# Later rows asked for sooner, twelve of sixteen weight conversions a step later, and the scores of two stacked blocks moved behind the products of the step ahead

## The chip, the cores and the metric

The kernel runs on one core of a Trainium2 chip. The time is that of one execution on the device, in microseconds, and the smaller one is the better one. The core has a matrix engine (TensorE, PE in the profile), a vector engine (VectorE, DVE), a scalar engine (ScalarE, ACT), a general engine (GpSimd, POOL) and a queue of DMA issues (SyncE, SP). Each of them runs its own list of instructions in order; they meet through semaphores.

## The reference

The reference is an attention with decay, followed by two layers of a feed-forward kind. What is computed, cut to what matters:

```python
# q, k, v: 4 batches, 8 heads, 576 positions, 64 wide; f: 4 x 8 x 576
scores = scale * np.matmul(q, k.transpose(0, 1, 3, 2))
cum = np.cumsum(np.log(np.clip(f, 0.0001, 1.0)), axis=-1)
scores = np.where(causal, -1e9, scores + cum[:, :, :, None] - cum[:, :, None, :])
attn = np.exp(scores - max); attn = attn / (sum + 1e-09)
x = attn @ v                                  # as 2304 tokens x 512
x = np.maximum(x @ w_in, 0.0) ** 2 @ w_out    # first layer pair, 2048 wide
h = x @ w_in2
out = np.where(h > 0, h, np.exp(np.minimum(h, 0)) - 1) @ w_out2
```

## The kernel before

The attention of batch 0 is computed in 20 steps (`todo`): eight steps of kind A, one for each head, for the first part of the positions; then for each pair of heads a step "4", in which the last 64 positions of both heads are stacked into one block of scores (`soft_4`), and two steps B for the positions between (`soft_b`). Each step has a front half, `soft`: scores on TensorE, a reduction on VectorE (`reduce_min`, L446), an exponential on ScalarE (`expo`, L449). Its back half, `outs`, comes one step later: transposes on TensorE (`pt`), a copy out of them (`e`, or `pp` for the steps B) and the products with the values (`pv`, one buffer, emptied by ScalarE into xA or xB). The blocks of `pp` are copied by ScalarE and VectorE in turns; the first product with the values needs the one of ScalarE.

Into the same steps the first feed-forward layer is woven (`moe_step`, `begin`, `unit`), a unit being 256 tokens. Unit 0 reads the tile x0, which the A steps fill; its products `ph<-x,w` are begun before all of x0 is there. Where no such work is at hand, matmuls of zeros (`busy`) are run. `fill` calls these between the pieces of a step.

The loop over i, at the end of the printed code, orders all this. In step i it does four things that matter here. It asks for rows of heads (`fetch_head`, which for batch 0 calls `fetch_plain`: one load of rows, one of values, one of augmented rows with the decay, all on SyncE's queue through `queued`) and for raw weights (`stage`), as the table BEGIN says: h is a head, w a weight, r the remaining decay rows. It converts weights, as many as W_AT[i] says: the raw weight is a pair of 32-bit words, made into a high and a low word by `words` and `load_w`, with two instructions on ScalarE (Abs, L157, and copy, L179) and five on VectorE (L159, L160, L161, L163 and the low word, L123). Sixteen halves are converted in all, the first-layer halves of the eight weight tiles first. Then it runs the two halves of the attention steps, with `fill` between their pieces.

What the code asks for is then put into a list for each engine by a scheduler, in which the calls `tc.issue_after(...)` hold an instruction behind another. So the order on an engine isn't that of the code, and is shown below for the places of the change.

Names in the profile: s is a bank of scores (two of them), rawA, rawB and rawC are rows of heads, e and eb the scores on their way, pt transposes, pv products with values, ph the first feed-forward products, g, gh, gl their squares in two words, w_0 to w_7 the weight tiles, wraw and raws_w their raw form, x1 the tokens in memory, xu the tile of a unit.

## Time and profile before

| | us |
|---|---|
| median of three runs (1026.98 to 1030.76) | 1026.98 |
| the profiled execution | 1025.79 |
| its span | 1024.0 |
| TensorE busy | 1011.2 |
| VectorE busy | 709.2 |
| ScalarE busy | 522.9 |
| GpSimd busy | 257.3 |

The span is what the profiler saw from the first to the last instruction; the time has 1.8 us more around it. The busy times are sums over the whole span. The attention of batch 0 and the first feed-forward units fill the first 190 us or so, and this change touches only that part. TensorE's waits are listed with the engine that the profile holds responsible for the end of the wait; where that engine had long been done, it was something else, often a DMA. The granted clock is given as a share of full speed.

### The profile page before, as it was taken

To read this page: it belongs to the slowest core of one execution; us is meant where nothing else is said; L and a number is where in the kernel's file an instruction comes from. 1 tells how busy PE (TensorE), PEld (TensorE's weight loads), DVE (VectorE), ACT (ScalarE), POOL (GpSimd) and SP (SyncE) were. 2 spreads that over 40 slices of the span, in tenths; PEclk is the share of its full clock that TensorE was granted. 3 is DMA by queue.
4 is the path that set the end of the run, shared out by engine and by line. 5 is a ranking of instruction groups with operands and counts; after the bars stand their busy time and mean duration, and the time that the engine had idled before them with its cause. 6 is when DMAs were issued, how large, how long until landed. Compare 5 with 4: busy or idle time off the path is not lost.

```text
span 1024.0 us, 17635 instructions
## 1 busy us (share of the span) xinstructions
PE 1011.2 (99%) x6363; PEld 899.2 (88%) x6363; DVE 709.2 (69%) x1595; ACT 522.9 (51%) x1196; POOL 257.3 (25%) x282
## 2 busy tenths in 40 slices
PE   9999999999999999999999999999999999999998
PEld 8777799899999988889988888998889988899997
DVE  8894788766775548845376779895455989654554
ACT  7674676766676634423243445553334555333331
POOL 2135697675774300012104040400000000000000
PEclk9999999999999999999999999999999999999999
DMA  8847547454531074443545645653415556353402
GB/s 212 271 140 208 171 137 227 146 153 124 183 106 62 24 259 125 143 132 116 175 139 211 210 169 197 234 178 113 145 42 185 165 186 207 102 182 126 147 21 83
DMA packets 77334, 157.59 MB, mean 154 GB/s; under 512 B 9616, under 2 KB 38032, under 8 KB 77248
## 3 DMA queue, kind: packets, MB, share of 16 engines
q1 hardware_dynamic: 77232, 156.46, 47.5%
q8 instruction: 50, 0.82, 0.3%
q14 instruction: 36, 0.29, 0.1%
q10 hardware_dynamic: 16, 0.02, 0.0%
HBM read 113.94 MB, written 38.90 MB: 149 GB/s over the span
## 4 chain that ended last, share of the span: by engine, by line
PE 95%; DVE 2%; DMA 1%; ACT 1%; POOL 1%; issue 0%; ACTq 0%; POOLq 0%; SPq 0%
PE O L192 33%; PE P L192 18%; PE pH L192 13%; PE ph L192 7%; PE o L192 6%; PE pt L513 5%; PE pv L520 4%; PE s L438 3%; PE pv L517 2%; PE s L442 2%; PE s L443 2%; PE idle L289 1%; DMA xu<-x 1%; PE pr L513 1%; DVE qk L131 0%
## 5 line engine op out<-in xcount | busy, mean ns | idle before, releaser
L192 PEld LDWEIGHTS P<-xu,v 128*128 128x128 f32 x1536 | 200.1, 189 | 10.8 <-issue 0.5
L192 PE MATMUL P<-xu,v 128*128 128x256 f32 x1536 | 203.7, 282 | 0.7 <-DMA xu<-x 0.7
L192 PE MATMUL O<-v,gh 128*128 128x512 f32 x576 | 171.1, 393 | 0.0
L192 PE MATMUL pH<-xu,w 128*128 128x512 f32 (+1 forms) x672 | 140.8, 360 | 0.0
L192 PEld LDWEIGHTS pH<-xu,w 128*128 128x128 f32 x672 | 114.0, 188 | 20.2
L192 PE MATMUL O<-gh,w 128*128 128x512 f32 (+1 forms) x448 | 122.6, 362 | 0.0
L192 PEld LDWEIGHTS O<-v,gh 128*128 128x128 f32 x576 | 102.8, 188 | 17.6
L1142 ACT ACTIVATE hs<-P 128x256 f32<-128x256 f32 x128 | 48.4, 381 | 113.8 <-PE P L192 113.0
L192 PE MATMUL O<-v,gl 128*128 128x512 f32 x288 | 103.5, 393 | 0.0
L192 PEld LDWEIGHTS O<-gh,w 128*128 128x128 f32 x448 | 79.8, 189 | 14.1
L136 POOL TENSOR_TENSOR yl<-pr,yh 128x512 fp32r<-128x512 f32 x18 | 25.1, 1394 | 248.5 <-ACT yh L962 174.7
L1145 DVE TENSOR_TENSOR hs<-P,hs 128x256 f32<-128x256 f32 x96 | 40.5, 422 | 62.2 <-PE P L192 58.9
L136 POOL TENSOR_TENSOR qk<-raw,qk 64x704 fp32r<-64x704 f32 (+1 forms) x48 | 77.1, 1606 | 17.6 <-DVE qk L131 5.2
L192 PE MATMUL O<-gl,w 128*128 128x512 f32 (+1 forms) x224 | 80.1, 363 | 0.0
L192 PE MATMUL o<-gh,w 128*128 128x256 f32 x384 | 76.1, 292 | 0.0
L157 ACT ACTIVATE wt<-wraw 128x512 f32<-128x512 f32 x57 | 38.4, 673 | 58.5 <-DMA wraw<-in_w_dram 39.4
L192 PE MATMUL ph<-xu,w 128*128 128x256 f32 x480 | 66.8, 287 | 0.3 <-DMA xu<-x 0.3
L682 ACT ACTIVATE gh<-g 128x512 fp32r<-128x512 f32 (+1 forms) x80 | 46.9, 586 | 38.2 <-DVE g L681 34.9
L681 DVE TENSOR_TENSOR g<-g 128x512 f32<-128x512 f32 (+1 forms) x56 | 45.1, 805 | 28.3 <-ACT g L677 28.1
L192 PEld LDWEIGHTS O<-v,gl 128*128 128x128 f32 x288 | 53.1, 188 | 10.3
L1113 ACT ACTIVATE gh<-g 128x512 fp32r<-128x512 f32 x72 | 45.4, 631 | 32.3 <-DVE g L1168 25.4
L192 PEld LDWEIGHTS o<-gh,w 128*128 128x128 f32 x384 | 60.3, 191 | 1.4 <-issue 0.5
(166 smaller groups left out, 2045.5 us busy)
## 6 DMA issues: line engine op xcount, KB each, us to landing
xu<-x SPq DMA_DIRECT2D x66, 512.0 KB
wraw<-in_w_dram SPq DMA_DIRECT2D x57, 512.0 KB
raw<-in_qkv_dram SPq DMA_DIRECT2D x24, 640.0 KB
x<-yh SPq DMA_DIRECT2D x31, 256.0 KB
x<-yl SPq DMA_DIRECT2D x31, 256.0 KB
x<-xs SPq DMA_DIRECT2D x16, 320.0 KB
xu<-x SPq DMA_DIRECT2D x16, 256.0 KB
rv<-in_qkv_dram SPq DMA_DIRECT2D x24, 160.0 KB
```

The source lines that it names most:

```text
L136: nc.gpsimd.tensor_tensor(out=dst, in0=x, in1=f32(hi), op=ALU.subtract)
L157: nc.scalar.activation(out=f32(t), in_=f32(hi), func=AF.Abs)
L192: nc.tensor.matmul(out=dst, lhsT=l, rhs=r, start=first and i == 0, stop=last and i == n - 1, skip_group_check=skip)
L438: seen[0] = nc.tensor.matmul(out=dst, lhsT=hh.t[0:68, hh.q + q0:hh.q + q0 + 128], rhs=hh.t[0:68, hh.k + j0:hh.k + j0 + n], start=first, st ...
L442: nc.tensor.matmul(out=dst, lhsT=qk1[:, q0:q0 + 128], rhs=qk1[:, QW + j0:QW + j0 + n], start=first, stop=False)
L513: seen[0] = nc.tensor.transpose(dst, src, ident[:, c0:c0 + 128])
L520: seen[0] = nc.tensor.matmul(out=dst, lhsT=hh[2][:, J, :], rhs=hl[i], start=first and i == 0, stop=last and i == 1)
L681: (nc.vector if sq == "v" else nc.gpsimd).tensor_tensor(out=g[:, 0:n], in0=g[:, 0:n], in1=g[:, 0:n], op=ALU.mult)
L682: nc.scalar.activation(out=gh[:, 0:n], in_=g[:, 0:n], func=AF.Copy)
L1113: nc.scalar.activation(out=gh, in_=g, func=AF.Copy)
L1142: nc.scalar.activation(out=o, in_=x, func=AF.Copy)
L1145: nc.vector.tensor_tensor(o, y, x, op=ALU.add)
```

## The change

It has six parts.

- BEGIN and `fetch_begin`: the load of the fifth raw weight goes behind the loads of the first two plain heads, and `fetch_plain` asks for the augmented rows of both heads before it asks for their values (`held`).
- W_AT: the first four conversions stay where they are, those of weights five to sixteen come a step or more later. `words` now holds the first instruction of those behind the last exponential that has been issued (`turned`).
- `soft_4`, first two pairs of batch 0: the scores are held behind the last matmul issued so far, and five matmuls of zeros are run ahead of them into the same bank.
- Zeros at the end of two score tiles are written at the start rather than in `block_zeros`.
- OPEN: at step 16 the tile of unit 1 is opened; `store_x` copies the later pairs of heads into it directly, and `load_x1` leaves these out.
- The raw weights' tile raws_w is allocated ahead of x0, so they trade buffers.

```diff
@@ -32,10 +32,10 @@
 
 W_MIN = float(np.uint32(0x38000000).view(np.float32))
 W_MAX = float(np.uint32(0x47EFFE00).view(np.float32))
-BEGIN = {0: "hh", 1: "w", 3: "whw", 4: "wrh"}
+BEGIN = {0: "hhw", 1: "w", 3: "whw", 4: "wrh"}
 PACE = (1.28, 0.9, 1.85, 1.75)
 COST = {'A': 0.7, '4': 1.1, 'B': 1.7}
-W_AT = (1, 1, 1, 1, 0, 0, 0, 0, 2, 2, 2, 2, 2, 2)
+W_AT = (1, 1, 1, 1, 0, 0, 0, 0, 0, 1, 2, 2, 2, 2, 2, 1)
 AHEAD = 2
 FETCH = 4
 LAG = 1
@@ -61,6 +61,7 @@
 
 WARM, FILL, FILL_TO = 47, 2, 9
 DELAY = 0
+OPEN = 16
 MEM = "gpsimd"
 WL = ('vv', 'vv')
 BUFS = {'raw': 3, 'qs': 3, 'vv': 4, 'ea': 2, 'eb': 3, 'p': 4, 't': 2, 'x': 1, 'xh': 1}
@@ -135,7 +136,7 @@
     def less(dst, x, hi):
         nc.gpsimd.tensor_tensor(out=dst, in0=x, in1=f32(hi), op=ALU.subtract)
 
-    reduced = []
+    reduced, turned = [], []
     staged = []
     at_step = [0]
     to_stage = [(fc, i) for i in range(2) for fc in range(8)]
@@ -153,7 +154,7 @@
     def words(raw):
         lo, hi = raw[:, :, 0], raw[:, :, 1]
         t = xa.tile([128, 512], I32, tag="o", name="wt")
-        with tc.issue_after(decays_made.ins):
+        with tc.issue_after((turned[-1] if at_step[0] > 8 else decays_made).ins):
             nc.scalar.activation(out=f32(t), in_=f32(hi), func=AF.Abs)
         with tc.issue_after(rows_made.ins):
             nc.vector.tensor_scalar(f32(t), f32(t), W_MIN, W_MAX, op0=ALU.max, op1=ALU.min)
@@ -210,8 +211,8 @@
 
     fr = ab.tile([32, S], F32, tag="eb", name="fr", bufs=BUFS["eb"])
     nc.sync.dma_start(out=fr, in_=f)
+    raws_w = xa.tile([128, 2, 512, 2], I32, tag="xu", name="raws_w")
     x0 = xa.tile([128, 2 * NC, CH], F32R, tag="xu", name="x0")
-    raws_w = xa.tile([128, 2, 512, 2], I32, tag="xu", name="raws_w")
     mz = a1.tile([128, 512], F32, name="mz")
     m4 = a1.tile([128, 288], F32, name="m4")
     ptA = [[a1.tile([128, 512], F32R, name=f"ptA{s}{t}") for t in range(2)] for s in range(2)]
@@ -223,6 +224,8 @@
     me.memset(f32(ca[:, 2:4, 0:256]), 1.0)
     nc.gpsimd.memset(mz, 0.0)
     mask(mz[:, 384:512], [[-1, 128]])
+    for s in range(2):
+        nc.gpsimd.memset(e4s[s][:, S:640], 0.0)
 
     halves = (slice(0, 256), slice(256, S))
     one = a1.tile([128, 1], F32, name="one")
@@ -264,8 +267,6 @@
     def block_zeros():
         quiet = nc.gpsimd.tensor_copy(go, f32(made[1][:, 1, S - 257:S - 256]))
         with tc.issue_after(quiet.ins):
-            for s in range(2):
-                nc.gpsimd.memset(e4s[s][:, S:640], 0.0)
             nc.gpsimd.memset(m4, 0.0)
             nc.gpsimd.tensor_copy(ident[:, 128:192], ident[:, 0:64])
             for k in range(2):
@@ -283,11 +284,12 @@
 
     begun = []
 
-    def busy(n):
+    def busy(n, into=None):
         for _ in range(n):
-            out = (begun[0] if begun else idle)[:, 0:256].rearrange("p (a b) -> p a b", a=2)
-            nc.tensor.matmul(out=out, lhsT=zero, rhs=zero.unsqueeze(1).broadcast_to([128, 2, 128]), start=not begun,
-                             stop=not begun, skip_group_check=bool(begun))
+            own = into is None and begun
+            out = (into if into is not None else begun[0] if begun else idle)[:, 0:256].rearrange("p (a b) -> p a b", a=2)
+            nc.tensor.matmul(out=out, lhsT=zero, rhs=zero.unsqueeze(1).broadcast_to([128, 2, 128]), start=not own,
+                             stop=not own, skip_group_check=bool(own))
 
     busy(WARM)
 
@@ -306,7 +308,7 @@
         nc.sync.dma_start(out=rv, in_=qkv[b, h, :, RAW:ALL])
 
     last_dma = [None]
-    rows = []
+    rows, held = [], []
 
     def queued(out, in_, hold=True):
         if last_dma[0] is None:
@@ -358,7 +360,6 @@
         decay(3)
         values(3)
         stage()
-        stage()
         aug_rows(False)
 
     def fetch_plain(b, h, part):
@@ -369,10 +370,11 @@
             t = hd.tile([128, RAW], F32, tag="qk1", name="rawC", bufs=BUFS["qs"])
             v = hd.tile([128, 5 * D], F32, tag="vv", name="vp", bufs=BUFS["vv"])
         queued(t[0:64, 0:ROW], plain[h])
-        queued(v, qkv[b, h, :, RAW:ALL])
         rows.append((t[64:68, 0:ROW], augb[h]))
-        while rows and h:
-            queued(*rows.pop(0))
+        held.append((v, qkv[b, h, :, RAW:ALL]))
+        for part_ in (rows, held) if h else ():
+            while part_:
+                queued(*part_.pop(0))
         raws[b, h, part] = Plain(t, 0, Q0, v.rearrange("p (j d) -> p j d", d=D))
 
     def late_rows():
@@ -446,7 +448,7 @@
         reduced.append(nc.vector.tensor_tensor_reduce(out=e, in0=s, in1=m, scale=-0.125, scalar=init, op0=ALU.add, op1=ALU.min, accum_out=nm))
 
     def expo(e, nm, z):
-        nc.scalar.activation(out=e, in_=e, func=AF.Exp, bias=nm, scale=-1.0, accum_out=z)
+        turned.append(nc.scalar.activation(out=e, in_=e, func=AF.Exp, bias=nm, scale=-1.0, accum_out=z))
 
     def invert(z, r):
         nc.vector.tensor_scalar(z, z, 1e-9, None, op0=ALU.add)
@@ -496,6 +498,9 @@
         nm0 = ab.tile([128, 1], F32, tag="nm0", name="nm0")
         for i in range(2):
             s = ps_s.tile([128, 512], F32, tag="s", name="s")
+            if not b and hp < 2 and not i:
+                with tc.issue_after(seen[0].ins):
+                    busy(5, s)
             c = slice(288 * i, 288 * i + 288)
             scores(s[:, 0:288], hhs[0], Q4, 288 * i, 288, True, False)
             scores(s[:, 0:288], hhs[1], Q4 - 64, 288 * i, 288, False, True)
@@ -544,6 +549,8 @@
             tr(pr[:, i * 128:i * 128 + 128], rb[:, i])
         nc.vector.tensor_tensor(x[:, c0:c0 + 256], x[:, c0:c0 + 256], pr[:, 0:256], op=ALU.mult)
 
+    second, here = [], set()
+
     def store_x(b, hp, x, c0, n):
         if b in SPLIT and c0 == 0:
             xs = x0[:, hp::NC]
@@ -554,6 +561,9 @@
         minus(ENG["xl"][b > 0], xs[:, 1, c], x[:, c], xs[:, 0, c])
         if not (b in SPLIT and c0 == 0):
             nc.sync.dma_start(out=x1[b][hp::NC, :, c0:c0 + n].rearrange("c p t -> p c t"), in_=f32(xs[:, :, c]))
+            if not b and second:
+                nc.sync.dma_start(out=f32(second[0][:, hp::NC, :]), in_=f32(xs[:, :, 0:CH]))
+                here.add(hp)
 
     def out_a(hh, e, x, k):
         pt = ps_t.tile([128, 512], F32, tag="t", name="pt")
@@ -695,8 +705,10 @@
         return gh, gl
 
     def load_x1(t0, n, pool):
-        x = pool.tile([128, 2 * NC, n], F32R, tag="xu", name="xu")
+        x = second[0] if t0 == CH else pool.tile([128, 2 * NC, n], F32R, tag="xu", name="xu")
         for c in range(NC):
+            if t0 == CH and c in here:
+                continue
             for off, step, b, s in runs(t0, n):
                 nc.sync.dma_start(out=f32(x[:, c::NC, off:off + step]), in_=x1[b][c::NC, :, s:s + step].rearrange("c p t -> p c t"))
         return x
@@ -912,6 +924,8 @@
             fill()
         if o and o[2] in "AB" and o[3]:
             stored[o[0]] += 1
+        if i == OPEN:
+            second.append(xa.tile([128, 2 * NC, CH], F32R, tag="xu", name="xu"))
     at.close()
 
     wb = pool(ctx, "wb", 1, "right")
```

TensorE, at the first scores of a stacked block. In the kernel before, the list reads so (x is the tile x0, zero the zeros):

```order
L513 MATMUL pt<-ident,e_1_137 128x128 x3
L192 MATMUL ph<-x_124,w_0_290 128x256 x2
L192 MATMUL ph<-x_124,w_2_337 128x256 x2
L438 MATMUL s<-rawC 128x288 x2
L192 MATMUL ph<-x_124,w_0_290 128x256
L192 MATMUL ph<-x_124,w_1_303 128x256 x3
L192 MATMUL ph<-x_124,w_2_337 128x256
L192 MATMUL ph<-x_124,w_3_391 128x256
L289 MATMUL ph<-zero 128x256 x7
```

In the changed kernel, at the same place:

```order
L518 MATMUL pt<-ident,e_1_137 128x128 x3
L193 MATMUL ph<-x_125,w_0_290 128x256 x2
L193 MATMUL ph<-x_125,w_2_337 128x256 x2
L193 MATMUL ph<-x_125,w_0_290 128x256
L193 MATMUL ph<-x_125,w_1_303 128x256 x3
L193 MATMUL ph<-x_125,w_2_337 128x256
L193 MATMUL ph<-x_125,w_3_391 128x256
L291 MATMUL ph<-zero 128x256 x7
```

The two scores from rawC are gone from between the products. They stand some 27 rows further on:

```order
L518 MATMUL pr<-ident,rb 128x128 x2
L522 MATMUL pv<-e_1_137,rawA 64x256
L522 MATMUL pv<-e_1_137,rawA 64x128
L522 MATMUL pv<-ea,rawA 64x256
L522 MATMUL pv<-ea,rawA 64x128
L291 MATMUL ph<-zero 128x256 x2
L291 MATMUL s<-zero 128x256 x5
L440 MATMUL s<-rawC 128x288 x4
L193 MATMUL ph<-x_125,w_0_290 128x256 x2
```

There the first stacked block is made in one piece of four matmuls, behind two pairs of products with the values that follow each other, and behind two and five matmuls of zeros. The lists of TensorE differ from here up to about 166 us and agree behind that.

TensorE, at the scores of the first B step (128x512 and 128x384). Before:

```order
L438 MATMUL s<-rawC 128x288 x2
L513 MATMUL pt<-ident,ea 128x128 x3
L438 MATMUL s<-rawC 128x512
L192 MATMUL ph<-x_124,w_0_290 128x256 x2
L192 MATMUL ph<-x_124,w_2_337 128x256 x2
L438 MATMUL s<-rawC 128x384
L192 MATMUL ph<-x_124,w_0_290 128x256
L192 MATMUL ph<-x_124,w_1_303 128x256 x3
L192 MATMUL ph<-x_124,w_2_337 128x256
L192 MATMUL ph<-x_124,w_3_391 128x256 x3
L289 MATMUL ph<-zero 128x256 x7
```

Changed, from the second of these pieces on:

```order
L440 MATMUL s<-rawC 128x384
L518 MATMUL pt<-ident,e_0_136 128x128 x3
L193 MATMUL ph<-x_125,w_0_290 128x256 x2
L193 MATMUL ph<-x_125,w_2_337 128x256 x2
L440 MATMUL s<-rawC 128x512
L193 MATMUL ph<-x_125,w_0_290 128x256
L193 MATMUL ph<-x_125,w_1_303 128x256 x3
L193 MATMUL ph<-x_125,w_2_337 128x256
L193 MATMUL ph<-x_125,w_3_391 128x256 x3
L440 MATMUL s<-rawC 128x384
L518 MATMUL pt<-ident,eb 128x128 x6
L522 MATMUL pv<-pp,vp 64x320
```

Between the second pair of these scores and the first product of pp with the values there stand now only transposes; in the kernel before, products and transposes of the last A steps and all scores up to the next pair of heads stood there.

ScalarE, at the exponentials of the same B step (eb). Before:

```order
L127 ACTIVATE xA<-pv 64x256
L157 ACTIVATE wt<-wraw_389 128x512
L449 ACTIVATE eb,zB<-eb,nm_672 128x512
L179 ACTIVATE w_6_650<-wt 128x512
L449 ACTIVATE eb,zB<-eb,nm_672 128x384
L127 ACTIVATE e_0_136<-e_0_136,r_602 128x576
L157 ACTIVATE wt<-wraw_426 128x512
L127 ACTIVATE xA<-pv 64x256
L127 ACTIVATE pp<-pt 128x320
```

Changed:

```order
L451 ACTIVATE eb,zB<-eb,nm_646 128x512
L451 ACTIVATE eb,zB<-eb,nm_646 128x384
L158 ACTIVATE wt<-raws_w 128x512
L180 ACTIVATE w_4_634<-wt 128x512
L687 ACTIVATE g<-ph 128x512
L451 ACTIVATE eb,zB<-eb,nm_683 128x512
L687 ACTIVATE g<-ph 128x512
L689 ACTIVATE g<-g 128x512
L128 ACTIVATE pp<-pt 128x320 x2
```

The copies and squares of the first unit (g) now stand ahead of the first copy pp, and the weight conversions at this place are those of w_4, which stood further up, ahead of the last A steps' exponentials.

## Rows read from the trace of the kernel before

**Rows 1.** The page, busy time (us), share of the span, instructions, of TensorE
```profile
PE 1011.2 (99%) x6363; PEld 899.2 (88%) x6363; DVE 709.2 (69%) x1595; ACT 522.9 (51%) x1196; POOL 257.3 (25%) x282
```

**Rows 2.** Waits of TensorE, 0 to 200 us: us in total, times, longest
```profile
PE s L442 <- DVE nm L446: 3.5, 4, 1.3
PE s L438 <- DVE wt L161: 1.7, 1, 1.7
...
PE pv L517 <- ACT xA L127: 0.6, 1, 0.6
PE ph L192 <- DMA xu<-x: 0.3, 1, 0.3
```

**Rows 3.** TensorE's timeline: start, us, line, operation, [idle before, releaser]
```profile
26.83 1.62 PE L438 MATMUL s<-rawC 68*128 68x288 f32 x4 [1.68 <-DVE wt L161]
...
33.28 0.86 PE L517 MATMUL pv<-e,rawA 128*64 128x256 f32 x4 [0.56 <-ACT xA L127]
...
35.39 0.49 PE L513 MATMUL pt<-ident,ea 128*128 128x128 f32 x3
35.72 1.02 PE L438 MATMUL s<-rawC 68*128 68x512 f32 x2
...
38.65 1.00 PE L289 MATMUL ph<-zero 128*128 128x256 f32 x7
...
51.62 2.27 PE L517 MATMUL pv<-pp,vp 128*64 128x320 f32 x10
...
85.52 0.40 PE L192 MATMUL o<-gh,w 128*128 128x256 f32 x2
...
121.19 0.35 PE L442 MATMUL s<-qk 128*128 128x256 f32 x1 [0.63 <-DVE nm L446]
...
146.99 0.44 PE L442 MATMUL s<-qk 128*128 128x384 f32 x1 [0.84 <-DVE nm L446]
```

**Rows 4.** Slices around the first stacked scores: length, busy of each engine, clock, DMA
```profile
26.00:27.00 1.00, 0.17 (x1) 0.20 (x2) 0.96 (x3) 0.44 (x3) 0.00 (x0) 1.00 0.90 311
27.00:28.00 1.00, 1.00 (x5) 0.75 (x4) 0.47 (x1) 0.00 (x0) 0.00 (x0) 0.75 1.03 418
28.00:29.00 1.00, 1.00 (x5) 0.85 (x5) 0.07 (x1) 0.77 (x2) 0.00 (x0) 0.50 1.15 332
...
30.00:31.00 1.00, 1.00 (x7) 1.00 (x7) 1.00 (x2) 0.00 (x0) 0.00 (x0) 0.55 1.08 256
```

**Rows 5.** Timeline of SyncE's queue
```profile
23.23 0.62 SPq L316 DMA_DIRECT2D rawC<-augb  x2
```

**Rows 6.** ScalarE's timeline
```profile
37.65 0.67 ACT L157 ACTIVATE wt<-wraw 128x512 f32<-128x512 f32 x1
...
40.05 0.76 ACT L127 ACTIVATE e<-e,r 128x576 f32<-128x576 f32 x1
...
42.73 0.44 ACT L127 ACTIVATE pp<-pt 128x320 f32<-128x320 f32 x1 [0.96 <-PE pt L513]
...
57.19 1.08 ACT L677 ACTIVATE g<-ph 128x512 f32<-128x512 f32 x2 [0.18 <-PE ph L192]
...
58.77 0.63 ACT L679 ACTIVATE g<-g 128x512 f32<-128x512 f32 x1
```

**Rows 7.** Slices of 16 us
```profile
24.00:40.00 16.00, 13.76 (x76) 11.07 (x75) 12.62 (x38) 10.70 (x29) 2.82 (x6) 0.89 0.97 297
40.00:56.00 16.00, 16.00 (x85) 10.96 (x84) 15.89 (x40) 13.13 (x32) 3.48 (x12) 1.00 0.72 198
```

**Rows 8.** VectorE's groups, 0 to 130 us: busy us, mean ns of one
```profile
L160 DVE TENSOR_SCALAR wt<-wt 128x512 int32<-128x512 int32 x16 | 9.4, 589 | 0.2
...
L446 DVE CUSTOM_DVE_ANT_0 eb<-s,mz 128x512 f32<-128x512 f32 x11 | 7.5, 682 | 1.7 <-PE s L438 1.2 <-PE s L443 0.5
```

**Rows 9.** VectorE's timeline
```profile
71.19 1.40 DVE L160 TENSOR_SCALAR wt<-wt 128x512 int32<-128x512 int32 x1
...
80.10 0.78 DVE L123 TENSOR_TENSOR w<-wt,w 128x512 fp32r<-128x512 f32 x1
```

## Prediction

> **What bounds the kernel now.** I read the busy shares first: TensorE is busy 1011.2 us, 99% of the span [rows 1]. Nothing that another engine does counts unless TensorE waits for it, and a change of order can win only TensorE's waits, TensorE's own additional work, and time at a lower clock. So the second view is TensorE's waits up to 200 us, the stretch that the change touches: 3.5 us for the score reductions in four waits, one wait of 1.7 before a score, 0.6 before a product with the values and 0.3 for a reload [rows 2]. The reader is to see how small this stock is: 6.1 us of 1024.
>
> The third view is TensorE's timeline, which says where each wait is: 1.68 us before the scores of the first stacked block at 26.83, 0.56 at 33.28, 0.63 at 121.19, 0.84 at 146.99 [rows 3]. The other two waits for a reduction stand behind 166 us, where the order of the matmuls is the same before and after; I leave them as they are. The wait at 26.83 is named after a weight conversion on VectorE. That name can't be right: the matmul has no operand from there. Its operand is the tile rawC, whose last piece, the augmented rows, SyncE issued at 23.23, 3.6 us earlier, behind two loads of values [rows 5]. I read it as the wait for these rows.
>
> The fourth view is the granted clock in slices of 1 us. Up to 27 us it is full; after the wait it is 0.75, 0.50, 0.50 (the slice not shown is like the one at 28) and 0.55, then 1.00 again [rows 4]. [...] The lost share of full speed is 0.25 + 0.50 + 0.50 + 0.45 = 1.7 us of work.
>
> **The change part by part.** The scores of the first stacked block leave the place at 26.83: there the order now goes on with the products of the step ahead, whose operands were there (they ran in the same place right behind the scores). That takes away the wait of 1.68. With it goes what stood in front of the fall of the clock, 1.7 us. Bounds: both go together, 3.4; or the clock was to fall for another reason and only 1.68 goes; or TensorE arrives sooner at the next product whose operand is late, and nothing goes, 0. I take 3.4, because the row shows an unbroken full clock up to this wait and again from 31 us on, through smaller waits [rows 3, 4].
>
> [...]
>
> Ten more matmuls of zeros are added, five ahead of each of the first two stacked blocks. They run on TensorE, beside nothing: 10 x 1.00 / 7 = 1.4 us [rows 3]. They would cost nothing only if TensorE had to wait there anyway; the rows of these two blocks, now asked for ahead of the values, are there some ten us before their new place, so I take 1.4 and keep 0 as the other end.
>
> The two products with the values, which in the row at 33.28 wait 0.56 for ScalarE to empty the one buffer they share, follow each other directly a second time in the new order. I take a second 0.56 [rows 3]; bounds 0 and, if ScalarE is at a 128x576 exponential, twice that, 1.1.
>
> The first two score blocks of the first pair of second parts (the pieces 512 and 384 wide) used to be hidden. Their first product with the values stood at 51.62, sixteen us behind the first score at 35.72, with other heads' work between [rows 3]. In the new order that work has been done earlier, and from the first 512-wide score to that product TensorE has: the score 1.02, the 384-wide one 0.77 (three quarters of it), nine transposes at 0.33 for three (35.39 to 35.72), and the second pair of scores with twelve products, 2.93 (35.72 to 38.65): 5.7 us [rows 3]. Against it the other engines have a chain, which I read from the new order of ScalarE: the score 1.02 and its reduction 0.68 [rows 3, 8]; two exponentials, one first step of a weight and one high word, 2.40 (37.65 to 40.05); another exponential, 0.60 (a quarter of that); two reads of the products' buffer with relu, 1.08; a square, 0.63; and the copy of the transposes that the product needs, 0.44 [rows 6]. That is 6.9 us. A new wait of 6.9 - 5.7 = 1.1 us (1.15 unrounded). Bounds: 0, if the second pair of scores is held up by an operand and the chain catches up meanwhile; 2.5, if the weight's high word waits for one stretched conversion of 1.40 on VectorE [rows 9]. A gain I exclude: no wait stood there. I take 1.1. This is the cover that the change uses up.
>
> The tile of the second token unit is opened earlier and half of it is filled without the way through memory. One wait of 0.29 for such a reload is in the trace [rows 2]; I take it as gone. The queue of SyncE loses two reloads and gets two copies in their place, and the fifth weight's load now stands behind the rows and values of two heads. That weight is needed when the first unit's third group begins, far later, so I cost it at nothing; the cover is the same as for the other weights, below.
>
> The weights. Twelve of sixteen conversions move a step later. Each takes VectorE five instructions of 128x512, 5 x 0.589 = 2.9 us [rows 8]; none is added. What changes is where they stand: before, VectorE was busy 12.62 of 16 us in 24 to 40 and 15.89 of 16 in 40 to 56 [rows 7]. Some three conversions, 8.8 us, leave the first stretch, which has room, for the second, which has none, so they push the later ones. The last of the sixteen ended at 80.10 + 0.78 = 80.9, and the last product of the first unit that uses it began at 85.5 [rows 3, 9]: 4.6 us of room. Following the new order with these durations I find the second-layer weights half a us to 2 us ahead of their products, since those products too stand later than before. I cost it at 0, with 4.2 (8.8 - 4.6) as the other end. That is the term I trust least.
>
> The moved zero fills on GpSimd and the order of the two buffers of x change no wait that the trace shows: 0.
>
> **The sum**: -1.68 - 1.7 - 0.29 + 1.4 + 0.56 + 1.1 = -0.6 us. The profiled execution took 1025.79 (span 1024.0 and 1.8 around it), the median of the runs is 1026.98. From the first I get 1025.2, from the second 1026.4; I forecast 1025.8, a change too small to be seen. A measurement of this kernel tells about 0.5%, 5 us, from no change.
>
> **Rivals.** *One, slower: VectorE comes too late with the weights.* The place is the second half of the first unit, from about 75 us on; it decides as soon as the shift is more than the 4.6 us of room. For it: the 15.89 of 16. And GpSimd's operations, which are denser there than in the stretch that the conversions leave, stretch VectorE's: the conversion at 71.19 took 1.40 where the mean of its sixteen is 0.589 [rows 8, 9]. The price is 4.2 us, or 6.6 with three such stretched instructions (3 x 0.8 more). -0.6 + 4.2 = +3.6 gives 1030.0, and with the stretching 1032.4. Against it: the order puts the products later too.
> [...]
>
> *Two: the new wait at the first product with the values brings the clock down*, as the old one did. For it: it is of the size of the one of 1.68. Against: 0.84 at 146.99 did not. Price 1.7: 1027.5.
>
> *Three: the waits go and none comes.* Nothing at the product, no second 0.56, and the waits of 0.56, 0.63 and 0.84 fall too: -1.68 - 1.7 - 0.29 - 2.03 + 1.4 = -4.3, 1022.1. For it: the later half of that stretch is reordered as well. Against: the four waits for reductions recur with the same pattern, in both orders.
>
> *Four: the change doesn't do what it says.* The wait moves to the next product, the clock falls as before, and 3.4 of the gain is missing: 1029.2. For it: a queue that is busy all the time. Against: the next products need only what the matmuls at 24 to 31 us had.
>
> **How the numbers follow.** My forecast 0.52 (its own range 1024 to 1028), rival one 0.16, two 0.10, three 0.15, four 0.07. The range goes from 1021.8, just under rival three, to 1031.0, into rival one; left out are the stretched case and what I have not thought of. Faster by over 0.5% (below 1021.9): 0.09, half of rival three. Slower by over 0.5% (above 1032.1): 0.07, the stretched half of rival one. Within 0.5%: 0.84.
>
> **What would show it.** No wait and no clock below 1.00 between 24 and 32 us: the first term is right. A wait of about a us before the first product of the copied transposes with the values, ended by ScalarE: the new term is right. Waits of TensorE for a weight in the second half of the first unit: rival one. TensorE's busy time should go up by 1.4 less the 1.7. I am wrong if TensorE waits for weights by more than 2 us, if the clock falls a second time, or if the later part, behind 166 us, moves by more than the shift at its start.

## The result and the profile after

The changed kernel took 1033.54 us (median of 10, 1030.75 to 1035.39), the kernel before 1026.98 (median of 10, 1024.33 to 1033.48): ratio 1.0051, 95% interval 1.0032 to 1.0070, by the ratio some 5 us slower (the medians lie 6.6 apart). The forecast was 1025.8 with a range to 1031.0. It was wrong, in the sign too. The profiled execution took 1035.39, the longest of the ten, and its span is 1033.6; the one of the kernel before took 1025.79, below its median. So the two traces lie 9.6 us apart, and they show where time goes better than how much the change costs.

The page of the changed kernel says, answering [rows 1]:

```profile
PE 1016.7 (98%) x6373; PEld 899.8 (87%) x6373; DVE 713.5 (69%) x1595; ACT 522.7 (51%) x1196; POOL 260.6 (25%) x282
```

TensorE is busy 5.5 us longer, and over the whole span it is also idle 4 us longer. The stretch in which the two orders differ can be measured exactly: it begins with the first product ph<-x,w, at 24.44 before [rows 3] and 25.04 after, and ends with a pair of transposes pr that stands at the same place of both lists. Of the kernel before, that row of TensorE's timeline and, as one slice (length, busy time and instructions of each engine, clock, DMA), the stretch:

```profile
171.04 0.38 PE L513 MATMUL pr<-ident,rb 128*128 128x128 f32 x2
```

```profile
24.44:171.04 146.60, 141.33 (x915) 114.99 (x914) 115.72 (x308) 98.76 (x254) 84.22 (x97) 0.99 0.62 188
```

Of the changed kernel, the same two:

```profile
178.01 0.38 PE L518 MATMUL pr<-ident,rb 128*128 128x128 f32 x2
```

```profile
25.04:178.01 152.97, 144.62 (x925) 114.27 (x924) 119.02 (x310) 98.90 (x255) 88.13 (x99) 1.00 0.59 184
```

146.60 us became 152.97: 6.4 us, of which 3.1 are more idle time (8.35 against 5.27) and 3.3 more busy time, though the stretch before held 1.7 us lost to the lower clock (0.50 to 0.75 in its slices from 27 to 31 us [rows 4]). Of the rest of the 9.6 us, 0.6 lie ahead of the stretch and 2.6 behind it. TensorE's waits in it, in the changed kernel (us in total, times, longest), against [rows 2]:

```profile
PE s L444 <- DVE nm L448: 1.8, 2, 1.6
PE pv L522 <- ACT pp L128: 1.7, 1, 1.7
PE s L444 <- DVE xB L534: 0.9, 1, 0.9
PE pv L522 <- ACT xA L128: 0.9, 2, 0.5
PE ph L193 <- DMA xu<-xs: 0.8, 1, 0.8
PE s L440 <- DVE nm L448: 0.8, 3, 0.3
PE pt L518 <- DVE p L515: 0.7, 1, 0.7
PE ph L193 <- ACT g L687: 0.4, 1, 0.4
PE o L193 <- ACT w L180: 0.2, 1, 0.2
```

The wait for the rows is gone. In its place stand a wait for the first copy pp, a second one for xA, and others that the stretch didn't have before: for reductions of rawB scores, for xB, for p, for the square g, for a weight w, and for the tile xu copied directly (before: 0.3 for its reload). The rows of TensorE's timeline that answer to [rows 3] (start, us, operation, idle time before and its releaser):

```profile
25.04 1.70 PE L193 MATMUL ph<-x,w 128*128 128x256 f32 x10
26.58 1.00 PE L291 MATMUL ph<-zero 128*128 128x256 f32 x7
...
29.63 0.86 PE L522 MATMUL pv<-e,rawA 128*64 128x256 f32 x4 [0.47 <-ACT xA L128]
...
35.38 0.86 PE L522 MATMUL pv<-ea,rawA 128*64 128x256 f32 x4 [0.46 <-ACT xA L128]
...
36.51 0.76 PE L291 MATMUL s<-zero 128*128 128x256 f32 x5
37.11 2.10 PE L440 MATMUL s<-rawC 68*128 68x288 f32 x8
...
46.69 0.82 PE L518 MATMUL pt<-ident,eb 128*128 128x128 f32 x6
49.16 0.75 PE L522 MATMUL pv<-pp,vp 128*64 128x320 f32 x2 [1.65 <-ACT pp L128]
...
54.66 0.85 PE L291 MATMUL s<-zero 128*128 128x256 f32 x5
```

From 25 us on the products run through without a wait, and seven zeros take 1.00 us: the clock is full there, 1.00 in each slice of 1 us from 24 to 50. The scores from rawC stand at 37.11 and don't wait. The two groups of five zeros take 0.60 and 0.69 to the next start, 1.3 in all. The wait of 1.65 is where the prediction put it. But here is what VectorE does meanwhile, in the changed kernel's timeline of VectorE:

```profile
25.44 0.81 DVE L124 TENSOR_TENSOR w<-wt,w 128x512 fp32r<-128x512 f32 x1
29.20 0.42 DVE L448 CUSTOM_DVE_ANT_0 ea<-s,mz 128x256 f32<-128x256 f32 x1 [2.95 <-PE pv L522]
...
35.43 0.42 DVE L550 TENSOR_TENSOR xA<-xA,pr 128x256 f32<-128x256 f32 x1 [4.28 <-ACT xA L128]
38.28 0.46 DVE L448 CUSTOM_DVE_ANT_0 e<-s,mz 128x288 f32<-128x288 f32 x1 [2.43 <-PE s L440]
...
41.27 0.43 DVE L160 TENSOR_SCALAR wt<-wt 128x512 f32<-128x512 f32 x1 [0.21 <-ACT wt L158]
```

From 26 to 41 us no conversion is begun, and scores to be reduced come only at 29.20 and from 38.28 on. VectorE stands still for most of 15 us. Two slices show that and what comes of it. Before, changed:

```profile
30.00:42.00 12.00, 11.44 (x63) 8.46 (x63) 10.04 (x30) 8.85 (x22) 1.33 (x3) 0.96 0.93 308
60.00:105.00 45.00, 45.00 (x276) 34.01 (x276) 30.47 (x67) 23.75 (x54) 23.10 (x24) 1.00 0.52 158
```

```profile
30.00:42.00 12.00, 11.45 (x72) 9.12 (x71) 2.77 (x11) 5.14 (x15) 2.05 (x4) 1.00 0.69 211
60.00:105.00 45.00, 43.64 (x226) 27.98 (x227) 42.78 (x97) 30.63 (x70) 21.17 (x20) 1.00 0.63 198
```

At 30 to 42 us VectorE works 2.77 of 12 us where it worked 10.04; at 60 to 105 it works 42.78 of 45 where it worked 30.47, and TensorE, which had no idle time there at all, loses 1.4 us.

The clock, against [rows 4], in slices of 1 us of the changed kernel:

```profile
196.00:197.00 1.00, 0.27 (x2) 0.21 (x2) 1.00 (x4) 0.47 (x3) 1.00 (x3) 1.00 0.65 143
197.00:198.00 1.00, 1.00 (x6) 1.00 (x6) 0.80 (x3) 0.42 (x2) 1.00 (x1) 0.60 0.96 364
198.00:199.00 1.00, 1.00 (x5) 1.00 (x5) 0.00 (x0) 0.00 (x0) 0.92 (x2) 0.50 0.80 254
```

The next slice is at 0.50 as well, the one at 200 us at 0.69, then it is full again. So the clock fell in this execution too and cost 1.7 us, only at 197 us instead of 27; and again a wait of TensorE stood in front of it (0.73 us, with 0.27 us of work in the first slice).

### The profile page after: what moved, and what is told of

It is laid out like the page before. It is cut to its first block, busy times and chain, and to the rows that moved or that the text cites. A ratio compares the mean times of both kernels' runs of the same rounds, so it can differ in the third digit from the quotient of the medians.

```text
span 1033.6 us, 17663 instructions
## 1 busy us (share of the span) xinstructions
PE 1016.7 (98%) x6373; PEld 899.8 (87%) x6373; DVE 713.5 (69%) x1595; ACT 522.7 (51%) x1196; POOL 260.6 (25%) x282
## 4 chain that ended last, share of the span: by engine, by line
PE 79%; DVE 11%; DMA 4%; issue 2%; ACT 2%; POOL 1%; SPq 0%; POOLq 0%; ACTq 0%; DVEq 0%
PE O L193 29%; PE P L193 15%; PE pH L193 11%; PE o L193 6%; PE ph L193 6%; PE pt L518 4%; PE pv L525 4%; PE s L444 2%; PE s L445 2%; DMA wraw<-in_w_dram 1%; DVE wt L164 1%; DVE wt L162 1%; DMA x<-yl 1%; PE pv L522 1%; DVE eb L448 1%
## 5 line engine op out<-in xcount | busy, mean ns | idle before, releaser
L137 POOL TENSOR_TENSOR qk<-raw,qk 64x704 fp32r<-64x704 f32 (+1 forms) x48 | 79.6, 1659 | 24.3 <-DVE qk L132 12.2
L193 PEld LDWEIGHTS ph<-xu,w 128*128 128x128 f32 x480 | 60.7, 190 | 1.1 <-DMA xu<-xs 1.0
```

The lines of the kernel that those rows point to most:

```text
L137: nc.gpsimd.tensor_tensor(out=dst, in0=x, in1=f32(hi), op=ALU.subtract)
L193: nc.tensor.matmul(out=dst, lhsT=l, rhs=r, start=first and i == 0, stop=last and i == n - 1, skip_group_check=skip)
```

## The experiments

Each was compared with executions of the kernel before on the same chip. Ratios are to those, with 95% intervals; the changed kernel's is 1.0051.

**u_weights**: the weights' times and their release as before, the rest changed.

```diff
-W_AT = (1, 1, 1, 1, 0, 0, 0, 0, 0, 1, 2, 2, 2, 2, 2, 1)
+W_AT = (1, 1, 1, 1, 0, 0, 0, 0, 2, 2, 2, 2, 2, 2)
-        with tc.issue_after((turned[-1] if at_step[0] > 8 else decays_made).ins):
+        with tc.issue_after(decays_made.ins):
```

> The changed kernel with the table of conversions and their release as before; all else changed. Theory W (the late conversions cost the time: they leave no products of w_4 to run while the first copy pp is made, and crowd VectorE later): the wait of 1.65 us before the first product of pp goes, the small waits for reductions of rawB scores and for a weight go, 1028 to 1029.5. Theory S (the place of the scores and their zeros cost it): at most 1.5 us come back, 1032 or more. The forecast's own sum has no cost in the weights: 1033.

Measured 1033.63, ratio 1.0063 (1.0038 to 1.0087). Nothing came back; theory W is out. The slices show why:

```profile
30.00:42.00 12.00, 8.23 (x40) 5.88 (x41) 9.55 (x22) 7.47 (x17) 2.58 (x4) 0.86 0.89 271
60.00:105.00 45.00, 45.00 (x256) 31.86 (x254) 33.33 (x79) 26.23 (x59) 18.94 (x19) 1.00 0.43 133
```

VectorE is busy again at 30 to 42 us and TensorE loses nothing from 60 to 105, but TensorE works only 8.23 of the first 12 us, part of them at a lower clock (0.86 over the slice). Its waits there, at 24 to 60 us:

```profile
PE pv L522 <- ACT xA L128: 3.4, 2, 2.9
PE pt L518 <- DVE pp L132: 1.8, 1, 1.8
```

With the scores held, the outputs of the A steps and the copies pp are all that TensorE has, and they stand behind the conversions on ScalarE and VectorE.

**u_scores**: the weights late, the rows early, the tile opened, but no hold and no zeros for the stacked blocks.

```diff
-            if not b and hp < 2 and not i:
-                with tc.issue_after(seen[0].ins):
-                    busy(5, s)
```

> The changed kernel without the hold and the ten zeros ahead of the first two stacked blocks' scores; weights late, rows early, tile opened. Theory S: zeros (1.2 us), the second wait for the one buffer of products (0.6) and the wait before pp (1.8) go: 1029 to 1030. If the rows, asked for earlier, are there at the early place, TensorE doesn't wait 1.68 us and the clock stays full there; if not, both are back and it is 1033. Theory W: within 1.5 us of the changed kernel.

Measured 1029.52, ratio 1.0015 (1.0001 to 1.0028). Most comes back: theory S. Its trace lists no wait for the rows of rawC, and the clock is 1.00 in all slices from 24 to 120 us. Its slices at two places:

```profile
30.00:42.00 12.00, 12.00 (x71) 8.98 (x70) 9.60 (x28) 9.65 (x26) 2.02 (x4) 1.00 0.88 269
60.00:105.00 45.00, 43.71 (x251) 30.88 (x250) 37.54 (x79) 24.92 (x55) 26.26 (x24) 1.00 0.57 182
```

What is left, 1.5 us, is about what TensorE still loses at 60 to 105 us (1.3), with VectorE at 37.54.

**u_open**: unit 1's tile opened and filled as before.

```diff
-OPEN = 16
+OPEN = -1
-        x = second[0] if t0 == CH else pool.tile([128, 2 * NC, n], F32R, tag="xu", name="xu")
+        x = second[0] if second and t0 == CH else pool.tile([128, 2 * NC, n], F32R, tag="xu", name="xu")
```

> The changed kernel with unit 1's tile opened and filled from memory as before. The wait for the copied tile (0.81 us at 127.67) goes back to some 0.3. Both theories: 0.5 us less, 1033, not to be told from the changed kernel. If the opened tile holds a buffer that the weights or outputs need, more: 1030.

Measured 1033.32, ratio 1.0057 (1.0037 to 1.0077): no difference, as both theories had it.

**u_fetch**: the loads in the order of before.

```diff
-BEGIN = {0: "hhw", 1: "w", 3: "whw", 4: "wrh"}
+BEGIN = {0: "hh", 1: "w", 3: "whw", 4: "wrh"}
...
+        queued(v, qkv[b, h, :, RAW:ALL])
         rows.append((t[64:68, 0:ROW], augb[h]))
-        held.append((v, qkv[b, h, :, RAW:ALL]))
-        for part_ in (rows, held) if h else ():
-            while part_:
-                queued(*part_.pop(0))
+        while rows and h:
+            queued(*rows.pop(0))
```

> The changed kernel with the order of the loads of before (fifth weight's load first, augmented rows behind the values). The scores stand so late in the new order that the rows are there anyway: no wait before them, clock full at 25 to 32 us. Theories W and S: same as the changed kernel within 1 us, 1033. If the order of the loads makes the 0.6 us by which the changed kernel is late at 25 us, 1032.5.

Measured 1037.82, ratio 1.0099 (1.0075 to 1.0124). A miss: 5 us dearer than the changed kernel. No wait for rows is in its trace; its executions had a lower mean clock, 0.9947 against 0.9976 for the kernel before beside them, which is 3 us of it. In the profiled execution, whose mean clock is 0.993, it is 1.00 from 80 to 88 us, 0.53 from 88 to 96 and 0.83 from 96 to 104. What the rest is I didn't find out.

**no_zeros**: the hold kept, put on the first score itself, without the ten zeros.

```diff
             if not b and hp < 2 and not i:
                 with tc.issue_after(seen[0].ins):
-                    busy(5, s)
+                    scores(s[:, 0:288], hhs[0], Q4, 288 * i, 288, True, False)
```

> The changed kernel with the first two stacked blocks' scores held behind the last matmul as in it, but without the ten matmuls of zeros. Theory Z (the zeros are the price: they and what the list makes of them): some 4 us come back, 1029.5. Theory P (the place is the price: the scores of the B step come right behind, and their chain of reduction, exponential, transposes and copies lies open on TensorE): only the zeros' own 1.2 us come back, 1032, and the waits before the first product of pp and for xA stay.

Measured 1036.37, ratio 1.0112 (1.0092 to 1.0133). Neither theory: without the zeros it is dearer. Theory Z is out. The wait before pp is there as ever (1.66), and the clock falls behind it, in the slices

```profile
42.00:48.00 6.00, 4.34 (x25) 2.99 (x24) 5.70 (x15) 5.42 (x14) 1.77 (x2) 0.99 0.98 294
48.00:54.00 6.00, 6.00 (x27) 3.54 (x25) 4.62 (x8) 3.26 (x7) 4.04 (x11) 0.73 0.40 122
```

where it didn't in the changed kernel (1.00 from 42 to 60 us). The mean clock of its executions is 0.9964, of the kernel before beside them 0.9991: some 2.8 of the 11 us. These are 5 executions.

**hold_second** and **hold_first**: hold and zeros for one of the two pairs of heads alone.

```diff
-            if not b and hp < 2 and not i:
+            if not b and hp == 1 and not i:
```

> The changed kernel with hold and zeros for the second pair of heads alone; the first block's scores are free to go early. Theory P for the first block (the wait of 1.65 us before pp and two of 0.6 for xA are at the first): most comes back, 1029.5 to 1030.5. If both blocks cost alike, half: 1031.5. If the second is the one: 1033.

> The changed kernel with hold and zeros for the first pair of heads alone. Theory P for the first block: little comes back, 1032.5. If both cost alike: 1031.5. If the second is the one: 1029.5.

For hold_first the condition is `hp < 1`. Measured: hold_second 1027.71, ratio 1.0023 (1.0010 to 1.0035); hold_first 1030.58, ratio 1.0054 (1.0037 to 1.0072). The first block is the price. In hold_first TensorE waits for weights at 60 to 105 us, as rival one had it:

```profile
PE o L193 <- DVE w L124: 2.6, 2, 1.4
```

The slices of hold_second and of hold_first:

```profile
30.00:42.00 12.00, 12.00 (x70) 9.02 (x71) 9.92 (x28) 9.20 (x24) 2.22 (x5) 1.00 0.81 252
60.00:105.00 45.00, 43.55 (x248) 30.40 (x246) 37.77 (x78) 24.67 (x59) 26.38 (x24) 1.00 0.63 187
```

```profile
30.00:42.00 12.00, 11.45 (x70) 8.98 (x70) 2.99 (x11) 4.81 (x11) 2.04 (x4) 1.00 0.73 223
60.00:105.00 45.00, 42.12 (x226) 27.02 (x224) 44.35 (x99) 28.75 (x67) 22.07 (x21) 1.00 0.61 186
```

With the first block's scores early, VectorE works 9.92 of 12 us, with them held 2.99. But TensorE's loss at 60 to 105 us isn't the hold's alone: hold_second, with the first block early, loses 1.45 there, and u_scores, with no hold, 1.29; in hold_first it is 2.88.

**d_scores**: hold and zeros added to the kernel before, with weights, rows and tile as they were (the five-line part of `soft_4` and `busy` with its second argument).

> The kernel before with the hold and the zeros alone added; rows, weights and tile as before. Theory P or Z (this part costs by itself): 1027.5 to 1028 plus 4 to 6, 1032 to 1034. Theory I (it costs only with the late weights, which no longer fill the place): within 1.5 us of the kernel before, 1029. The run with the weights back as before speaks against I.

Measured 1035.32, ratio 1.0096 (1.0079 to 1.0114). The hold costs by itself, and more than the whole change does, whose interval ends at 1.0070. Its slices:

```profile
30.00:42.00 12.00, 8.69 (x54) 6.78 (x52) 9.93 (x21) 6.67 (x16) 2.51 (x4) 1.00 0.92 299
60.00:105.00 45.00, 45.00 (x257) 31.26 (x255) 27.40 (x73) 24.43 (x56) 17.23 (x18) 1.00 0.48 143
```

VectorE isn't idle here and isn't behind later; it is TensorE that works only 8.69 of 12 us, as in u_weights.

**pp_vector**: the first copy pp by VectorE.

```diff
-CP = {'pA': 'a', 'pB': 'av', 'xA': 'a', 'xB': 'a'}
+CP = {'pA': 'a', 'pB': 'va', 'xA': 'a', 'xB': 'a'}
```

> The changed kernel, the copies pp shared out the other way round: the first one by VectorE, the second by ScalarE. The order then also puts six products of w_4 ahead of the first product of pp. Theory P (the open chain behind the first held scores is the price): the wait of 1.65 us shrinks to under 0.5 and 1.5 to 2 us come back, ratio to the kernel before 1.0035. Theory V (held scores leave VectorE and ScalarE idle at 30 to 42 us, and the work they owe makes VectorE late from 60 to 105 us): the wait goes, but the time is given back later, ratio 1.005 as for the changed kernel.

Measured 1033.62, ratio 1.0073 (1.0050 to 1.0095). Theory P's 1.5 us didn't come. But the run tells less than it should, since the wait wasn't taken away. The longest of its waits at 24 to 60 us:

```profile
PE pt L518 <- ACT pp L128: 1.7, 1, 1.7
```

TensorE now waits the same 1.7 us, before a transpose, for the copy that ScalarE makes.

**light_after** and **light_before**: the changed kernel and the kernel before, both of which leave out the clamp and the lowest bits of the weights 5 to 16 (two of VectorE's five instructions for each).

```diff
-        with tc.issue_after(rows_made.ins):
-            nc.vector.tensor_scalar(f32(t), f32(t), W_MIN, W_MAX, op0=ALU.max, op1=ALU.min)
+        if not 3 < n_words[0] < 16:
+            with tc.issue_after(rows_made.ins):
+                nc.vector.tensor_scalar(f32(t), f32(t), W_MIN, W_MAX, op0=ALU.max, op1=ALU.min)
...
+        n_words[0] += 1
+        if not 4 < n_words[0] < 17:
+            with tc.issue_after(reduced[min(1, len(reduced) - 1)].ins):
+                nc.vector.scalar_tensor_tensor(t, lo, 29, t, op0=ALU.logical_shift_right, op1=ALU.bitwise_or)
```

> The changed kernel, which leaves out two of VectorE's five instructions for weights 5 to 16 (the clamp and the lowest bits): 24 instructions of about 0.6, 14 us less for VectorE. Theory V: VectorE catches up by 60 us, waits from 60 to 105 us go: 3 to 5 us come back, ratio 1.001 to 1.002. Theory P: no more than the wait before pp, which products of w_4 then cover, 1.9 us: 1.0035.

> The kernel before, with the same 24 instructions of VectorE left out. TensorE waits there for VectorE only from 120 us on, when the conversions are over. Theory V holds if this one gains clearly less than the changed kernel does: ratio 0.999 to 1.0. If it gains as much (0.996), VectorE's load costs in either order and the comparison says nothing of the change.

Measured: light_after 1028.03, ratio 1.0011 (0.9989 to 1.0034); light_before 1028.02, ratio 1.0008 (0.9987 to 1.0029). Less work for VectorE gives back 4 us to the changed kernel and nothing to the one before, as theory V has it. The slices of light_after:

```profile
30.00:42.00 12.00, 11.46 (x69) 8.86 (x68) 3.48 (x12) 5.03 (x12) 1.90 (x4) 1.00 0.58 196
60.00:105.00 45.00, 45.00 (x260) 32.54 (x260) 30.43 (x71) 27.07 (x64) 19.98 (x22) 1.00 0.59 176
```

VectorE stands as idle at 30 to 42 us as in the changed kernel, but what it owes is small enough: at 60 to 105 it is where it was before, and TensorE works all 45 us. The products of w_4 also come early enough to stand ahead of the first product of pp, and that wait is gone as well; so this run doesn't part the two places from each other.

**d_fetch**: the order of the loads alone, on the kernel before (the edits of u_fetch, the other way round).

> The kernel before with the order of the loads of the changed one (augmented rows ahead of values, fifth weight behind two heads) and nothing else: the scores stay early, the rows are there. The wait of 1.68 us at 26.83 goes: ratio 0.998. If the fall of the clock hung on that wait, 1.7 more: 0.9967. If the fall comes anyway at another place, the mean clock of the executions is the same as for the kernel before.

Measured 1028.60, ratio 1.0013 (0.9991 to 1.0034). The wait of 1.68 is gone, and the clock is full there (1.00 in the slices 24 to 30 and 30 to 36 us), in TensorE's timeline:

```profile
26.57 1.13 PE L438 MATMUL s<-rawC 68*128 68x288 f32 x4
...
28.26 1.00 PE L289 MATMUL ph<-zero 128*128 128x256 f32 x7
```

and still nothing is gained. Of its waits at 24 to 180 us, these are new or have grown:

```profile
PE ph L192 <- DMA xu<-x: 1.1, 1, 1.1
PE pv L517 <- DVE pp L131: 0.6, 1, 0.6
```

The first was 0.3 before. With 0.4 for xB, what is new comes to about the 1.68 that went; all waits of that stretch are 5.6 us, against 5.3 in the kernel before. VectorE works 12.00 of the 12 us from 30 to 42 here, and TensorE loses 1.18 at 60 to 105. The mean clock of the executions is 0.9982, of the kernel before beside them 0.9983: no clock is won either. In the profiled execution it is 1.00 in all slices from 24 to 120 us, and its mean is 0.998, the same as in the profiled one of the kernel before: what is lost lies at another place.

**pad_early** and **pad_late**: 20 idle instructions of VectorE in the kernel before.

```diff
+        if i == 8:
+            last_pad = reduced[-1]
+            for _ in range(20):
+                with tc.issue_after(last_pad.ins):
+                    last_pad = nc.vector.tensor_scalar(mz, mz, 1.0, None, op0=ALU.mult)
```

> The kernel before, with 20 idle instructions of VectorE (the mask times 1, 128x512, about 0.4 us each, 8 us) added between the conversions from some 34 us on; nothing held, no zeros. It puts VectorE behind by about as much as its idle time at 30 to 42 us does in the changed kernel. Theory V: TensorE waits from 60 to 105 us and the time rises by 3 to 6 us, ratio 1.003 to 1.006. If VectorE's lateness isn't the cause: 1.000.

> The same 20 instructions, added behind the last conversions, at some 85 to 100 us, where VectorE has room. Theory V: no more than 1 us, ratio 1.000 to 1.001. If any 8 us on VectorE costs, as much as the early ones.

For pad_late, i is 19. Measured: pad_early 1053.32, ratio 1.0256 (1.0230 to 1.0281); pad_late 1036.78, ratio 1.0084 (1.0053 to 1.0115). Both miss by far. The added instructions did not just run beside the others: the order around them changed, and pad_early got two waits of a length that no other kernel has,

```profile
PE s L438 <- DVE nm L446: 8.1, 1, 8.1
PE ph L192 <- POOL x L136: 5.5, 2, 5.2
```

and 0.985 of the clock. In pad_late the instructions stand from 98 to 113 us, later than meant, and TensorE waits 2.9 us there for a reduction. Neither run speaks for theory V or against it: the early ones cost 26 us where it has 3 to 6, and the late ones 8.6 where it has at most 1.

**light_d_scores**: d_scores, with the same instructions left out as in light_after.

> The kernel before with hold and zeros (ratio 1.0096) that leaves out the clamp and the lowest bits for weights 5 to 16, 14 us less for VectorE. Here the weights aren't moved. Theory V for the hold as such: 4 us or more come back, ratio below 1.006. If the hold's price lies in the waits for the one buffer of products and for the unit's tile (3.8 us in that run's trace), which VectorE's load doesn't touch: 1.008 or more.

Measured 1031.45, ratio 1.0041 (1.0022 to 1.0060), against 1.0096: some 5.6 us back, in a kernel whose weights aren't moved. Less work for VectorE helps there too, as theory V for the hold as such has it, but not by way of 60 to 105 us, where d_scores loses nothing. 4 us stay, and its trace has the waits for xA (3.2 us) that the expectation named.

No version was faster than the kernel before.

## Why the prediction was wrong

The terms of the sum, and what the stretch of the profiled execution shows in their place:

| term | forecast | measured |
|---|---|---|
| wait for the rows | -1.68 | -1.68 |
| clock | -1.7 | -1.7 here, +1.7 at 197 us |
| tile xu | -0.29 | +0.52 (0.81 for 0.29) |
| ten zeros | +1.4 | +1.3 |
| second wait for xA | +0.56 | +0.37 (0.93 for 0.56) |
| wait before pp | +1.1 | +1.65 |
| late weights and VectorE, 60 to 105 us | 0 | +1.35 |
| waits behind 120 us, without xu | 0 | +0.78 |
| below what the profile lists as a wait | not thought of | +3.7 |

The measured ones add up to 6.3 of the 6.4 us, clock at 197 left out; the last line is the remainder.

The table is that of one execution of each kernel. What the parts cost is better read from the ratios, and there the failed step is plain. u_scores has every part of the sum that was to gain (no wait before the scores from rawC, a clock of 1.00 behind them, the tile) and the late weights too, but not the hold and its zeros. For these parts the forecast was -1.68 - 1.7 - 0.29 + 0 = -3.7 us; measured is +1.5 (0.1 to 2.9). The hold and the zeros were forecast at 1.4 + 0.56 + 1.1 = 3.1; measured is 3.7 (1.0051 less 1.0015, each known to 1.5 or 2 us). So the price was nearly right, and the gain was not there.

Step one, the wait for the rows, failed: it goes, but nothing is won by it. d_fetch takes it away by the order of the loads alone and isn't faster: 1.0013, and its interval begins at 0.9991, while 1.68 us would be 0.9984 and 3.4 would be 0.9967. Its other waits grow by as much. The bound that I had named and passed over, "TensorE arrives sooner at the next product whose operand is late, and nothing goes, 0", is what the run shows. The sign that I had asked for, no wait and a full clock from 24 us on, came nearly as named (one wait of 0.47, at 29.63), and was no sign of a gain. That VectorE, busy 12.00 of 12 us there, is what makes those operands late is my reading; no run shows it for this order.

Step two, the clock, failed with it. I took one profiled execution, saw the fall behind the wait, and made that one wait the cause. A mean clock of 0.998 or less (the two profiled executions, each with one such fall, have 0.998) is in 5 of the 10 executions of the changed kernel and in 46 of 84 of the kernel before. The mean over the executions is 0.9987 after, and 0.9976 to 0.9991 for the kernel before on four occasions; there was nothing to gain. A second profile at the outset would have cost this term its place.

Step three, the zeros, the second wait for xA and the wait before pp: right in kind and place. The last came to 1.65 us, half as much again as forecast. ScalarE's chain was the one named, with the square and both reads of the products ahead of pp.

Step four, the late weights at 0, left something out. I moved three conversions out of a stretch "which has room", asked whether the weights would come in time for their products, and found that they did; they do, the only wait for one is of 0.17. I didn't ask what VectorE would do in the emptied stretch. The hold took the scores' reductions and all that follows from the same stretch in which the conversions were taken away, so VectorE went idle there, 2.77 of 12 us, and was behind until 105 us. TensorE waits then for reductions, a square and a weight, 1.35 us. How much of this is the price of the late weights isn't shown: u_scores loses 1.29 in the same 45 us without the hold, and d_fetch 1.18 with neither hold nor late weights. No run has the late weights alone; u_scores (1.0015) and d_fetch (1.0013) can't be told apart. Rival one named the engine; in the changed kernel the weights don't come late, in hold_first they do (2.6 us).

u_weights and u_scores part the hold from the weights: with the hold, the weights may stand early or late, the time is the same within the intervals (1.0063, 1.0051). Early, TensorE has nothing to do at 30 to 42 us; late, VectorE hasn't. So the hold makes some 3.7 of the 5.2 us, and hold_first (1.0054) and hold_second (1.0023) put it at the first block. Its work, the scores, feeds a chain through three engines, and it was put ten us later (26.83 to 37.11) to spare TensorE 1.68. That VectorE's load then makes it dear is what light_after bears out: with less work for VectorE the changed kernel gets 4 us back, and the kernel before none. Its order of products moved a little as well, so the load isn't the only thing that differs. At which wait the price falls depends on the rest of the order: before pp in the changed kernel, at weights in hold_first, for xA in u_weights and d_scores.

Rival two had the clock fall behind the new wait. In the changed kernel it didn't (1.00 from 48 to 60 us, behind the wait of 1.65); in no_zeros and pp_vector it was lower behind a wait of the same length (0.73 at 48 to 54 us behind 1.66, 0.86 at 48 to 60 behind 1.7). Why it falls behind one wait and not behind another of that length, no run here shows.

Open: the 3.7 us in the last line of the table. About 1.1 of it, by an estimate, is that the matmul ahead of a wait doesn't overlap with the next one: in the kernel before, three transposes at 35.39 took 0.49 and the next matmul began 0.33 behind their start, at 35.72 [rows 3]. The six transposes at 46.69 end at 47.51, where by that row the next matmul would have started 0.16 sooner, and there are 13 such waits against 6, so 7 x 0.16. The other 2.6 us stand in no list of waits, and I couldn't place them. In light_after TensorE's busy time over the same stretch is 142.43 against 144.62, so most of them go when VectorE has less to do. Open too is why the waits behind 120 us grew by 0.78, and what makes the order of the loads worth 5 us in u_fetch and nothing in d_fetch.

## What to carry to other kernels

A wait taken from the busiest engine is a gain only as far as the operands behind it are there sooner too; here 1.68 us went and the time stayed. Try the cheapest way to take it away alone (the order of two loads, in this case) before paying for another. Before moving an operation to a later place because its operand is late, add up what every engine has to do in the place it leaves and in the one it goes to, with all the edits of the change together: work of a chain that is held is idle time for some engine, and here it came back as lateness. And don't book a fall of the clock as the price of the wait in front of it from one execution; look whether it is at the same place in a second one.

## What the runs showed of the hardware

The granted clock was lower for some time in most of the profiled executions, at places that differ. In slices of 1 us it was 0.50 to 0.75 from 27 to 31 us in the kernel before and 0.50 to 0.69 from 197 to 201 in the changed one. In longer slices it was 0.72 at 30 to 36 us in light_d_scores, 0.73 there in u_weights, 0.53 at 36 to 42 in light_before, 0.73 at 48 to 54 in no_zeros, 0.86 at 48 to 60 in pp_vector, 0.50 at 60 to 75 in pad_early, 0.53 at 88 to 96 in u_fetch and 0.77 at 105 to 120 in pad_late. The mean of the profiled execution was 0.998 or less in 14 of 17; in hold_second, hold_first and d_scores it was 1.000, 0.999 and 0.999, though these have waits of 1.6, 1.4 and 1.5 us. In the two kernels compared a wait of TensorE stood in front of the fall, of 1.68 us before and 0.73 after; a wait of 1.65 in the changed kernel, at 47.51, was followed by 1.00. With the wait of 1.68 taken away the mean clock over the executions stayed the same (d_fetch 0.9982, the kernel before 0.9983).

Whether matmuls of zeros hold the clock up isn't shown. The changed kernel, with ten of them (1.3 us of work), had a mean clock of 0.9987 and no_zeros 0.9964; but u_fetch, u_weights and d_scores, with the same ten, had 0.9947, 0.9970 and 0.9975.
